# One load for the first K, beta and masks, V's scaling behind the first solve, later loads chained by copies, and another clock model in a self-ordered linear-attention and MoE kernel

## The chip, the cores and the metric

The kernel runs on one core of one Trainium2 chip. TensorE (PE) does the matmuls and loads their weights (PEld), VectorE (DVE, V in the code), ScalarE (ACT, A) and GpSimd (POOL, G) do the rest, and SyncE (SP) issues the DMAs. The metric is device time in microseconds, the median of several runs. The profile is of one further execution.

## The reference

Two parts follow each other: a delta-rule linear attention over 4 batches, 8 heads, 768 tokens and head size 48, and a gated feed-forward layer on its result.

```python
k_n = k / (norm(k) + 1e-6)
state = zeros(B, H, 48, 48)
for t in range(768):
    y[t] = q[t] @ state                      # read before the update
    v_old = state.T @ k_n[t]
    state += beta[t] * outer(k_n[t], v[t] - v_old)
x = y.transpose(0, 2, 1, 3).reshape(3072, 384)
out = ((x @ w_a) * (x @ w_b)) @ w_out        # 384 -> 1536 -> 384
```

## The kernel before

**Attention.** The 768 tokens are cut into 24 chunks (c) of 32, and four chunks make a group (g = 0 to 5). All 32 heads of a chunk are worked on together: 128 partitions hold four blocks of 32 tokens, and eight column blocks hold the rest. For each group there are three generators. `prep(g)` loads K (tile `knb`), the transposed keys and queries (`rawb`, from `in_kqt`) and V (`vnb`) of two pairs of chunks, squares K for its norms, forms `dc` (beta over the norm), multiplies keys with keys and queries for each chunk (the Gram matmuls `bank<-rawb`), writes the scaled Gram blocks into `gnat` (tile `b4`, shown as `b`) and the masked key-query products into `at`; then it sums squares of V and of the keys and queries for a power-of-two scale (`sc`, with one matmul against `ones`), and multiplies V by the norms (`vnb<-vnb,nm`). `solve(g)` transposes the Gram blocks and eliminates on VectorE, step by step (`tmp<-b,b`, then `b<-b,tmp`), transposes the result (`b`, `xn`), and in groups 0 and 1 completes it on TensorE (`bank<-b,tt`, `bank<-b,mk`, `wr`, `bank<-wr,xn`) into `tt`. `steps(g)` goes through the chunks: state times keys and queries (`bank<-sh,rawb`), `f` = V minus that, `u` from `tt` and `f`, the state update `S_ps<-u,knb`, and the outputs `bank<-u,at`, which become `y`, are transposed (`yt`) and split into two half-precision parts (`xb`).

**MoE.** `weights(i)` loads one of 12 blocks of the layer's weights (`in_w`, 1.15 MB) into `late` or a part of `wh` that is free, unpacks it on VectorE (one TENSOR_SCALAR and two SCALAR_TENSOR_TENSOR of 128x1152), forms a power-of-two scale (`sw`, with ScalarE's square and one matmul against `ones`), and writes high and low halves; for blocks 0 to 3 the low halves come from TensorE (`zi`, `neg`, `negr`). `moe(s, fcs)` then does a MoE unit for a pair of chunks s and a block fc: 18 matmuls `bank<-xb,wh`, ScalarE's copy `a`, the product `g`, its two halves `ghl`, and six matmuls `bank<-wo,ghl`. There are 12 pairs and 12 blocks, so 144 units.

**Order.** No instruction is issued while this code runs. Each call is recorded as an `Op` by a `Plan` (hence one line, 481, for nearly all rows of the profile), and `Plan.pack` then lists the operations: an engine takes the ready operation of highest priority, with priorities from six passes forwards and backwards. The planner's rules matter here: `price` gives durations, `fetch` models TensorE's instruction fetch in blocks of 256, a window of 3,413 ns models its clock (`warm`, `use`), and before 60 us gaps on TensorE are filled with idle matmuls on `ones` (line 472): small ones of 128x32 and large ones of 128x256, which the trace shows as two passes each. `plan.behind` puts an operation behind named others in the plan alone. Engines are in-order, so what stands ahead in an engine's list is waited for.

**Loads.** `EARLY` and `NEXT` give the first loads. In `NEXT`, a GpSimd copy of one element from an earlier load's target into the next one's makes the second DMA wait for the first one's landing. In groups 2 to 5 the loads of a group were only ordered in the plan.

Of the kernel before, what the change touches and what calls it, by code (L numbers as in the profile page):

```python
# [42 lines left out]

EARLY = [(0, "k"), (2, "k"), (0, "r"), (0, "b")]
NEXT = [(2, "r", 0, "k"), (0, "v", 0, "r"), (2, "v", 2, "r"), (0, "w", 2, "r"), (1, "w", 0, "v"), (2, "w", 2, "v"), (4, "k", 0, "w"), (4, "r", 1, "w"), (4, "v", 2, "w")]
QUEUE = [(0, [0, 1, 2, 3, 4, 5]), (1, [0, 1, 2, 3, 4, 5]), (0, [6, 7, 8]), (1, [6, 7, 8]), (0, [9, 10, 11]), (1, [9, 10, 11])]
# [14 lines left out]
class Plan:  # L61
# [131 lines left out]
    def add(self, eng, fn, name, args, kw):  # L193
# [73 lines left out]
    def pack(self, pri, back=False):  # L267
# [17 lines left out]
        while len(done) < n:  # L285
# [59 lines left out]
            if e == "PE" and not back:  # L345

                if kept:
                    f, end = max(free[e], self.SINCE), min(t - self.SHY, slow.get(i, t))
                    room = end - f
                    fill[i], best_ = [0, 0], None  # L350
                    for lot in range(int(room / self.IDLE[0]) + 1 if room > 3000.0 else 1):
                        p_, c_, f_, m = pos, come, f, 0
# [7 lines left out]
                    while True:  # L360
                        k = 0 if fill[i][0] + 1 <= n_small else 1
                        while until <= f:
                            warm = use > 0.43 * self.WINDOW if warm else use > 0.75 * self.WINDOW
                            use, until = 0.0, until + self.WINDOW
                        took = self.IDLE[k] * (1 if warm or not k else 2)
                        slip, past, then = self.fetch(f, 2 + 2 * k, took, pos, come, dma)
                        if slip > 1.0 or f + took > end:
                            break
                        use, f, pos, come = use + took, f + took, past, then
                        fill[i][k] += 1  # L370
                _, pos, come = self.fetch(t, o.words, o.dur if warm else o.cold, pos, come, dma)
                while until <= t:
                    warm = use > 0.43 * self.WINDOW if warm else use > 0.75 * self.WINDOW
                    use, until = 0.0, until + self.WINDOW
                took = o.dur if warm else o.cold
                full = took * o.use / o.dur
                part = min(1.0, (until - t) / took)
                use += full * part
                if part < 1.0:
                    warm = use > 0.43 * self.WINDOW if warm else use > 0.75 * self.WINDOW  # L380
                    use, until = full * (1 - part), until + self.WINDOW
# [28 lines left out]
    BEGIN, IDLE, SINCE, UNTIL = 63, (50.0, 440.0), 1200.0, 60e3  # L410
    SHY, AIM = 400.0, 56

    def fetch(self, t, n, took, pos, come, dma):
        slip, come = 0.0, come[:]
# [69 lines left out]
@with_exitstack  # L484
def tile_kernel(ctx, tc, kqt, kn, vn, beta, w, masks, out):
    nc = tc.nc
# [51 lines left out]
    rawb = one("rawb", [P, 6, 1024])  # L538
    knb = one("knb", [P, 6, 384])
    vnb = one("vnb", [P, 6, 384])  # L540
# [26 lines left out]

    mk = one("mk", [P, 32 + P + 2])
    parity = mk[:, 32 + P :]
    bt = one("bt", [P, NG * 32])  # L570
    amask = mk[:, 0:32]
# [108 lines left out]
    def target(c, what):  # L680
        t = {"b": lambda: bt, "w": lambda: slots[c].bitcast(F32), "k": lambda: knp(c)[:, 0], "v": lambda: vnp(c)[:, 0], "r": lambda: rawp(c)[:, 0]}
        return t[what]()[0:1, 0:1]

    def load(c, what):
# [3 lines left out]
        if what == "w":  # L688
            SP.dma_start(slots[c].rearrange("p (n d) -> p n d", n=4), w[c].bitcast(I32)[:, :, 0 : WB // 4])
        elif what == "b":  # L690
            SP.dma_start(bt, beta)
            SP.dma_start(mk, masks)
        elif what == "k":
            SP.dma_start(knp(c).rearrange("p c d -> p (c d)"), kn[c // 2])
        elif what == "v":
            SP.dma_start(vnp(c).rearrange("p c d -> p (c d)"), vn[c // 2])
        else:
            SP.dma_start(rawp(c).rearrange("p c (h d) -> p (c h) d", h=2), kqt[c // 2][:, :, 0:512])

    def prep(g):  # L700
        chs = GROUPS[g]
        ss = sst
        if g > 1:
            last = []
            for c in chs[2], chs[0]:
                for what in "krv":
                    plan.behind = set(last)
                    load(c, what)
                    last = [len(plan.ops) - 1]
        for c in chs[::2]:  # L710
# [22 lines left out]
        for ci, c in enumerate(chs):  # L733
# [21 lines left out]
            ats[c] = atr()  # L755
            V.tensor_mul(ats[c], ga[:, :, 32:64], amask.unsqueeze(1).broadcast_to([P, 8, 32]))
            yield
        sc = scr()
        V.memset(sc[:, 0:4], 0.0)
# [13 lines left out]
        if g:  # L773
            V.tensor_add(sc[:, 2:3], sc[:, 2:3], vsum[-1])
        V.tensor_add(sc[:, 2:3], sc[:, 2:3], sc[:, 3:4])
        V.tensor_add(sc[:, 0:1], sc[:, 0:1], sc[:, 1:2])
        vsum.append(sc[:, 2:3])
# [12 lines left out]
        for ci, c in enumerate(chs):  # L790
            facs[c] = fac
            (V if g < 2 else G).tensor_mul(
                vnc(c).rearrange("p (q e) -> p q e", e=D),
# [5 lines left out]
    def solve(g):  # L799
# [5 lines left out]
        V.transpose(dtt, dcs[g])  # L805
        X = b4().rearrange("p (a b) -> p a b", b=32)
        (G if g else V).memset(X, 0.0)
        V.tensor_copy(X.rearrange("p t s -> p (t s)")[:, 0 : 33 * 31 + 1 : 33], dtt)
# [306 lines left out]
def _layout(inputs):  # L1115
# [25 lines left out]
    for j in range(3):  # L1141
# [12 lines left out]
    wide = np.zeros((NFC, P, 4, 288 + 8), w.dtype)  # L1154
    wide[..., 0:288] = w.reshape(NFC, P, 4, 288)
    return {
        "kqt": pieces,
        "kn": f(natl(k)),
        "vn": f(natl(v)),
        "beta": f(bp.reshape(P, NG * 32)),  # L1160
        "w": wide.view(np.int64),
        "masks": masks,
    }
# [17 lines left out]
```

## Time and profile before

| what | value |
|---|---|
| median of 3 runs | 656.05 us (653.93 to 656.95) |
| profiled execution, its own time | 659.53 us |
| its span, first to last instruction | 657.5 us |
| mean granted TensorE clock | 0.984 |
| PE busy | 626.8 us (95%) |
| VectorE busy | 406.5 us (62%) |
| idle matmuls on `ones` | 165 records, 22.1 us |

The page shows busy time by engine, then 40 slices of 16.4 us each with busy tenths, granted clock (PEclk, 9 is 90% or more) and DMA. "Idle before, releaser" is the time an engine waited ahead of a row and what ended it; "issue" means nothing that the profile shows. A matmul of 32-bit floats counts as two matmuls and two weight loads.

### The profile page before, as it was taken

To read this page: it belongs to the slowest core of one execution; us is meant where nothing else is said; L and a number is where in the kernel's file an instruction comes from. 1 tells how busy PE (TensorE), PEld (TensorE's weight loads), DVE (VectorE), ACT (ScalarE), POOL (GpSimd) and SP (SyncE) were. 2 spreads that over 40 slices of the span, in tenths; PEclk is the share of its full clock that TensorE was granted. 3 is DMA by queue.
4 is the path that set the end of the run, shared out by engine and by line. 5 is a ranking of instruction groups with operands and counts; after the bars stand their busy time and mean duration, and the time that the engine had idled before them with its cause. 6 is when DMAs were issued, how large, how long until landed. Compare 5 with 4: busy or idle time off the path is not lost.

```text
span 657.5 us, 26749 instructions
## 1 busy us (share of the span) xinstructions
PE 626.8 (95%) x12297; PEld 534.1 (81%) x12297; DVE 406.5 (62%) x1059; ACT 271.7 (41%) x599; POOL 21.4 (3%) x34
## 2 busy tenths in 40 slices
PE   6899989999899999979999999999999989999997
PEld 5766778788788888868888788888888877888886
DVE  5888898876468974337974348954449844332222
ACT  3257854354374443314543326453322253332322
POOL 0000000000021100000200001100000000000000
PEclk9879999999899999979999999999999999999999
DMA  7848042024143000033000051000000000000000
GB/s 249 315 147 329 6 140 81 3 77 167 62 162 115 1 25 4 13 129 114 1 25 4 4 202 50 1 26 3 4 3 25 1 27 4 2 25 1 25 1 25
DMA packets 19985, 42.78 MB, mean 65 GB/s; under 512 B 1185, under 2 KB 4513, under 8 KB 19873
## 3 DMA queue, kind: packets, MB, share of 16 engines
q1 hardware_dynamic: 19872, 41.08, 17.7%
q8 instruction: 96, 1.57, 1.0%
q14 instruction: 17, 0.13, 0.1%
HBM read 36.36 MB, written 4.72 MB: 62 GB/s over the span
## 4 chain that ended last, share of the span: by engine, by line
PE 76%; DVE 15%; ACT 4%; issue 3%; DMA 2%; SPq 0%; POOL 0%; ACTq 0%; DVEq 0%
PE bank L481 70%; DVE b L481 5%; DVE tmp L481 3%; PE S_ps L481 3%; PE bank L472 2%; DVE ghl L481 2%; DVE g L481 1%; ACT tt L481 1%; DMA rawb<-in_kqt 1%; ACT ghl L481 1%; ACT sqf L481 1%; DMA vnb<-in_vn 1%; DVE f L481 0%; DVE late L481 0%; ACT a L481 0%
## 5 line engine op out<-in xcount | busy, mean ns | idle before, releaser
L481 PEld LDWEIGHTS <-wh 128*128 128x128 f16 x2592 | 242.8, 99 | 54.4 <-issue 24.3
L481 PE MATMUL bank<-xb,wh 128*128 128x256 f16 x2160 | 262.0, 275 | 4.8 <-issue 3.5
L481 PE MATMUL bank<-wo,ghl 128*128 128x384 f32 x864 | 191.5, 355 | 1.0 <-issue 1.0
L481 PEld LDWEIGHTS bank<-wo,ghl 128*128 128x128 f32 x864 | 145.1, 191 | 5.1 <-issue 1.2
L481 ACT COPY a<-bank 128x256 f32<-128x256 f32 x144 | 53.6, 372 | 202.0 <-PE bank L481 201.5
L481 DVE TENSOR_TENSOR g<-bank,a 128x256 f32<-128x256 f32 x144 | 60.6, 421 | 121.4 <-ACT a L481 120.5
L481 ACT CAST ghl<-g 128x256 fp32r<-128x256 f32 x144 | 58.1, 404 | 76.3 <-DVE g L481 75.8
L481 DVE TENSOR_TENSOR ghl<-g,ghl 128x256 fp32r<-128x256 f32 x144 | 62.5, 434 | 37.7 <-ACT ghl L481 35.3
L481 DVE TENSOR_TENSOR b<-b,tmp 128x31 f32<-128x31 f32 (+20 forms) x154 | 51.9, 337 | 3.1
L481 PE MATMUL bank<-late,wh 128*128 128x256 f16 x432 | 53.1, 273 | 0.1
L481 DVE TENSOR_TENSOR tmp<-b,b 128x31 f32<-128x31 f32 (+20 forms) x154 | 50.9, 331 | 2.9
L481 DVE SCALAR_TENSOR_TENSOR y<-bank,sc,y 128x384 f32<-128x384 f32 x23 | 14.2, 617 | 42.4 <-ACT y L481 40.9
L481 PE MATMUL bank<-rawb 48*32 48x64 f32 x1280 | 25.2, 236 | 9.0 <-DMA rawb<-in_kqt 4.9
L481 PEld LDWEIGHTS bank<-rawb 48*32 48x32 f32 x1280 | 22.1, 119 | 13.5 <-issue 5.8
L481 ACT COPY sh<-S_ps 112x768 f32<-112x768 f32 x23 | 18.4, 798 | 22.8 <-PE S_ps L481 22.6
L481 PEld LDWEIGHTS bank<-sh,rawb 48*64 48x64 f32 x1216 | 19.7, 134 | 6.2 <-issue 3.8
L481 PE MATMUL bank<-sh,rawb 48*64 48x48 f32 x1216 | 22.3, 220 | 1.6 <-issue 1.6
L481 PE MATMUL bank<-u,at 32*32 32x48 f32 x1536 | 21.8, 203 | 1.6 <-issue 1.6
L472 PE MATMUL bank<-ones 128*32 128x32 bf16 (+1 forms) x165 | 22.1, 292 | 1.1 <-DVE ones L481 1.1
L481 PEld LDWEIGHTS bank<-f,tt 32*32 32x32 f32 x1472 | 17.4, 105 | 6.8 <-issue 2.7
L481 PEld LDWEIGHTS bank<-u,at 32*32 32x32 f32 x1536 | 18.3, 105 | 4.8 <-issue 4.0
L481 PEld LDWEIGHTS S_ps<-u,knb 32*48 32x48 f32 x1216 | 16.2, 123 | 7.3 <-issue 4.2
(118 smaller groups left out, 538.3 us busy)
## 6 DMA issues: line engine op xcount, KB each, us to landing
late<-in_w SPq DMA_DIRECT2D x10, 1152.0 KB, 7.6
rawb<-in_kqt SPq DMA_DIRECT2D x10, 1024.0 KB, 7.9
out<-late SPq DMA_DIRECT2D x24, 192.0 KB, 1.9
knb<-in_kn SPq DMA_DIRECT2D x10, 384.0 KB, 6.5
vnb<-in_vn SPq DMA_DIRECT2D x10, 384.0 KB, 6.1
wh<-in_w SPq DMA_DIRECT2D x2, 1152.0 KB, 10.1
late<-in_kqt SPq DMA_DIRECT2D x2, 1024.0 KB, 6.2
late<-in_kn SPq DMA_DIRECT2D x2, 384.0 KB, 3.1
```

Source lines behind the costliest of these rows:

```text
L472: self.nc.tensor.matmul(self.pool[-1][0 : 32 + 96 * k, 0 : 32 + 224 * k], one, one.unsqueeze(1).broadcast_to([P, 1 + k, 32 + 96 * k])[:, 0 ...
L481: fn(*(self.place(a, lease) for a in args), **{k: self.place(a, lease) for k, a in kw.items()})
```

## The change

It has five parts. K of chunks 0 and 1, beta and the masks come in one load of 1,122 floats a partition into one tile `kb`, which also holds the later K; the second key-query load is gated by the second K instead of the first. In group 0 `prep` is split: the masked product `at` of chunk 3, the norm's sums, `sc` and V's scaling are put behind the first solve's last transpose, by generators and `plan.behind`. In groups 2 to 5 each load is chained to the one before it by a GpSimd copy, and the key-query loads are cut into halves (`r0`, `r1`). The planner's clock model counts use by the part of the array that a matmul fills, with thresholds `KEEP` and `GAIN` and other idle rules (`SHY`, `HEAT`). `fetch` no longer judges a block that it has only just added.

```diff
-EARLY = [(0, "k"), (2, "k"), (0, "r"), (0, "b")]
-NEXT = [(2, "r", 0, "k"), (0, "v", 0, "r"), ...
+EARLY = [(0, "k"), (2, "k"), (0, "r")]
+NEXT = [(2, "r", 2, "k"), (0, "v", 0, "r"), ...
...
-                op.use += dur
+                n = 1
+                for d in outs[0].shape[1:]:
+                    n *= d
+                k, m, f = ins[0].shape[0] / 128, ins[0].shape[-1] / 128, ins[0].dtype == F32
+                op.use += (1 + 3 * f) * n / 2.4 * m * (k + 1) / 2 + 5 * f
...
-                    for lot in range(int(room / self.IDLE[0]) + 1 if room > 3000.0 else 1):
+                    for lot in range(max(1, int((room - 4000.0) / self.IDLE[0]))):
...
-                            warm = use > 0.43 * self.WINDOW if warm else use > 0.75 * self.WINDOW
+                            warm = use > (self.KEEP if warm else self.GAIN) * self.WINDOW
...
-    SHY, AIM = 400.0, 56
+    SHY, KEEP, GAIN, HEAT = 1500.0, 0.41, 0.42, (3.0, 430.0)
...
-            slip = max(slip, come[b] - at)
+            if b < known:
+                slip = max(slip, come[b] - at)
...
-        elif what == "b":
-            SP.dma_start(bt, beta)
-            SP.dma_start(mk, masks)
+        elif what == "k" and c == 0:
+            SP.dma_start(kb[:, 0 : begin.shape[1]], begin)
...
-                for what in "krv":
-                    plan.behind = set(last)
-                    load(c, what)
-                    last = [len(plan.ops) - 1]
+                for part in "k", "r0", "r1", "v":
+                    if (c, part[0]) in loaded and part != "r1":
+                        continue
+                    if last:
+                        G.tensor_copy(target(c, part), target(*last))
+                    load(c, part)
+                    last = c, part
...
+        if g == 0:
+            yield
+            plan.lease.update(rest[1])
+            plan.behind = set(ready)
+            rest[0]()
...
+            plan.behind = set() if g else set(ready)
             (V if g < 2 else G).tensor_mul(
...
+        if g == 0:
+            ready[:] = [len(plan.ops) - 1]
+            yield
...
+    for _ in range(6):
+        next(pr[0])
+    for _ in range(4):
+        next(sv[0])
     run_all(pr[0])
     next(ws[0])
-    for _ in range(3):
-        next(sv[0])
```

TensorE, from the last of the 97 small idle matmuls up to the first solve's result (`b_3_71`), before: 

```order
L472 MATMUL bank_66<-ones 128x256
L481 MATMUL bank_61<-rawb 32x64 x32
L481 MATMUL bank_62<-rawb 32x64 x32
L481 MATMUL bank_63<-rawb 32x64 x32
L481 MATMUL bank_64<-rawb 32x64 x32
L472 MATMUL bank_66<-ones 128x256 x6
L481 MATMUL bank_65<-sc_129,ones 128x1 x2
L472 MATMUL bank_66<-ones 128x256 x21
L481 MATMUL bank_61<-b_3_71,tt_85 32x16 x32
```

The same place after, from TensorE's first instruction:

```order
L477 MATMUL bank_66<-ones 128x256 x6
L486 MATMUL bank_61<-rawb 32x64 x32
L486 MATMUL bank_62<-rawb 32x64 x32
L486 MATMUL bank_63<-rawb 32x64 x32
L486 MATMUL bank_64<-rawb 32x64 x32
L477 MATMUL bank_66<-ones 128x256 x20
L486 MATMUL bank_65<-b_3_71,tt_85 32x16 x32
L486 MATMUL bank_61<-b_3_71,tt_86 32x16 x32
L486 MATMUL bank_62<-sc_127,ones 128x1 x2
```

The small idle matmuls are gone, six large ones stand ahead of the Gram blocks, and the norm's product (`sc`) has moved behind the first two blocks of the solve's result.

VectorE, from the Gram block of chunk 2 to the first elimination steps, before:

```order
L481 TENSOR_TENSOR b_0_68<-bank_62,dc_124 128x8x32
L481 TENSOR_TENSOR at_78<-bank_62,mk 128x256
L481 TENSOR_TENSOR vnb<-vnb,nm_126 128x384 x2
L481 TENSOR_TENSOR b_0_68<-bank_63,dc_124 128x8x32
L481 TENSOR_TENSOR at_79<-bank_63,mk 128x256
L481 TENSOR_TENSOR b_0_68<-bank_64,dc_124 128x8x32
L481 TENSOR_TENSOR at_80<-bank_64,mk 128x256
L481 TENSOR_TENSOR sc_129<-sc_129 128x1
L481 TENSOR_TENSOR vnb<-vnb,nm_126 128x384 x2
L481 STREAM_TRANSPOSE b_1_69<-b_0_68 128x1024
L481 TENSOR_TENSOR sc_129<-sc_129 128x1
L481 TENSOR_TENSOR tmp<-b_1_69,b_2_70 128x30
```

And after:

```order
L486 TENSOR_TENSOR b_0_68<-bank_62,dc_122 128x8x32
L486 TENSOR_TENSOR at_78<-bank_62,kb 128x256
L486 TENSOR_TENSOR b_0_68<-bank_63,dc_122 128x8x32
L486 TENSOR_TENSOR at_79<-bank_63,kb 128x256
L486 TENSOR_TENSOR b_0_68<-bank_64,dc_122 128x8x32
L486 STREAM_TRANSPOSE b_1_69<-b_0_68 128x1024
L486 TENSOR_TENSOR tmp<-b_1_69,b_2_70 128x30
```

Both pairs of V's scalings, chunk 3's `at` and the sums of `sc` have left this stretch; they follow the solve's transposes, ahead of the first weights (`wh<-late`).

SP, the loads of groups 2 and 3 behind the last weights (`late<-in_w`), before:

```order
L481 DMA late<-in_kn 128x768
L481 DMA late<-in_kqt 128x4x512
L481 DMA late<-in_vn 128x768
L481 DMA knb<-in_kn 128x768
L481 DMA rawb<-in_kqt 128x4x512
L481 DMA vnb<-in_vn 128x768
L481 DMA knb<-in_kn 128x768
```

And after, where each waits for a copy on POOL:

```order
L486 DMA late<-in_kn 128x768
L486 DMA late<-in_kqt 128x2x512 x2
L486 DMA kb<-in_kn 128x768
L486 DMA late<-in_vn 128x768
L486 DMA rawb<-in_kqt 128x2x512
L486 DMA kb<-in_kn 128x768
L486 DMA rawb<-in_kqt 128x2x512 x2
```

The key-query loads have become halves, and the loads of group 3 (the first `kb<-in_kn`) now stand between those of group 2.

More of the change, by code (lines that the diff above doesn't have):

```diff
@@ L368, in pack @@
                             break
-                        use, f, pos, come = use + took, f + took, past, then
+                        use, f, pos, come = use + self.HEAT[k], f + took, past, then
                         fill[i][k] += 1
@@ L372, in pack @@
                 while until <= t:
-                    warm = use > 0.43 * self.WINDOW if warm else use > 0.75 * self.WINDOW
+                    warm = use > (self.KEEP if warm else self.GAIN) * self.WINDOW
                     use, until = 0.0, until + self.WINDOW
                 took = o.dur if warm else o.cold
-                full = took * o.use / o.dur
+                full = o.use
                 part = min(1.0, (until - t) / took)
@@ L379, in pack @@
                 if part < 1.0:
-                    warm = use > 0.43 * self.WINDOW if warm else use > 0.75 * self.WINDOW
+                    warm = use > (self.KEEP if warm else self.GAIN) * self.WINDOW
                     use, until = full * (1 - part), until + self.WINDOW
@@ L410 @@
     BEGIN, IDLE, SINCE, UNTIL = 63, (50.0, 440.0), 1200.0, 60e3
-    SHY, AIM = 400.0, 56
+    SHY, KEEP, GAIN, HEAT = 1500.0, 0.41, 0.42, (3.0, 430.0)
     def fetch(self, t, n, took, pos, come, dma):
-        slip, come = 0.0, come[:]
+        slip, come, known = 0.0, come[:], len(come)
         for b in range(-(-pos // 256), -(-(pos + n) // 256)):
             at = t + took * (b * 256 - pos) / n
-            slip = max(slip, come[b] - at)
+            if b < known:
+                slip = max(slip, come[b] - at)
             if b + 1 == len(come):
@@ L484, in tile_kernel @@
 @with_exitstack
-def tile_kernel(ctx, tc, kqt, kn, vn, beta, w, masks, out):
+def tile_kernel(ctx, tc, kqt, kn, vn, begin, w, out):
     nc = tc.nc
@@ L538, in tile_kernel @@
     rawb = one("rawb", [P, 6, 1024])
-    knb = one("knb", [P, 6, 384])
+    kb = one("kb", [P, NG * 32 + 32 + P + 2 + 6 * 384])
+    bt = kb[:, 0 : NG * 32]
+    mk = kb[:, NG * 32 : NG * 32 + 32 + P + 2]
+    knb = kb[:, NG * 32 + 32 + P + 2 :].rearrange("p (c d) -> p c d", d=384)
     vnb = one("vnb", [P, 6, 384])
@@ L566, in vnc @@
         return vnp(c // 2 * 2)[:, c % 2]
-    mk = one("mk", [P, 32 + P + 2])
     parity = mk[:, 32 + P :]
-    bt = one("bt", [P, NG * 32])
     amask = mk[:, 0:32]
@@ L680, in target @@
     def target(c, what):
-        t = {"b": lambda: bt, "w": lambda: slots[c].bitcast(F32), "k": lambda: knp(c)[:, 0], "v": lambda: vnp(c)[:, 0], "r": lambda: rawp(c)[:, 0]}
+        t = {"w": lambda: slots[c].bitcast(F32), "k": lambda: knp(c)[:, 0], "v": lambda: vnp(c)[:, 0], "r": lambda: rawp(c)[:, 0], "r0": lambda: rawp(c)[:, 0], "r1": lambda: rawp(c)[:, 1]}
         return t[what]()[0:1, 0:1]
@@ L696, in load @@
             SP.dma_start(vnp(c).rearrange("p c d -> p (c d)"), vn[c // 2])
-        else:
-            SP.dma_start(rawp(c).rearrange("p c (h d) -> p (c h) d", h=2), kqt[c // 2][:, :, 0:512])
+        elif what == "r":
+            SP.dma_start(rawp(c).rearrange("p c (h d) -> p (c h) d", h=2), kqt[c // 2][:, :, 0:512])
+        else:
+            i = int(what[1])
+            loaded.add((c, "r"))
+            SP.dma_start(rawp(c)[:, i].rearrange("p (h d) -> p h d", h=2), kqt[c // 2][:, 2 * i : 2 * i + 2, 0:512])
     def prep(g):
@@ L755, in prep @@
             ats[c] = atr()
-            V.tensor_mul(ats[c], ga[:, :, 32:64], amask.unsqueeze(1).broadcast_to([P, 8, 32]))
-            yield
+            if c == 3:
+                rest = partial(V.tensor_mul, ats[c], ga[:, :, 32:64], amask.unsqueeze(1).broadcast_to([P, 8, 32]))
+                rest = rest, {t.tensor.name: plan.lease[t.tensor.name] for t in [ga]}
+            else:
+                V.tensor_mul(ats[c], ga[:, :, 32:64], amask.unsqueeze(1).broadcast_to([P, 8, 32]))
+            yield
+        if g == 0:
[3 more added lines that the diff above has]
+            rest[0]()
         sc = scr()
@@ L774, in prep @@
             V.tensor_add(sc[:, 2:3], sc[:, 2:3], vsum[-1])
+        plan.behind = set() if g else set(ready)
         V.tensor_add(sc[:, 2:3], sc[:, 2:3], sc[:, 3:4])
+        plan.behind = set() if g else set(ready)
         V.tensor_add(sc[:, 0:1], sc[:, 0:1], sc[:, 1:2])
@@ L791, in prep @@
             facs[c] = fac
+            plan.behind = set() if g else set(ready)
             (V if g < 2 else G).tensor_mul(
@@ L806, in solve @@
         X = b4().rearrange("p (a b) -> p a b", b=32)
+        plan.behind = set(ready if g else ())
         (G if g else V).memset(X, 0.0)
@@ L1155, in _layout @@
     wide[..., 0:288] = w.reshape(NFC, P, 4, 288)
+    nat = f(natl(k))
     return {
         "kqt": pieces,
-        "kn": f(natl(k)),
+        "kn": nat,
         "vn": f(natl(v)),
-        "beta": f(bp.reshape(P, NG * 32)),
+        "first": f(np.concatenate([bp.reshape(P, NG * 32), masks, nat[0]], axis=1)),
         "w": wide.view(np.int64),
-        "masks": masks,
     }
```

2 lines of the change are left out of this document (1 added, 1 removed).

## The prediction

> **What bounds the kernel now.** First the page: how long, which engine, at what clock.
>
> ```profile
> span 657.5 us, 26749 instructions
> PE 626.8 (95%) x12297; PEld 534.1 (81%) x12297; DVE 406.5 (62%) x1059; ACT 271.7 (41%) x599; POOL 21.4 (3%) x34
> PEclk9879999999899999979999999999999999999999
> q8 instruction: 96, 1.57, 1.0%
> ```
>
> TensorE is the bound over the whole span. The change can therefore gain only where TensorE idles, repeats idle work, or runs at a lower clock: 30.7 us of idle, and the slices with digits 7 and 8. The last row counts 96 fetches of 16 KB for PE's 24,594 instructions, 256 to each. Next the stages of the beginning (PE, PEld, DVE, ACT, POOL busy, then granted clock, DMA share, GB/s):
>
> ```profile
> 0.00:9.80 9.80, 3.92 (x99) 3.17 (x99) 3.95 (x9) 3.40 (x5) 0.38 (x5) 1.00 0.81 267
> ...
> 33.30:65.00 31.70, 29.48 (x831) 20.26 (x831) 27.00 (x52) 20.58 (x43) 1.04 (x1) 0.89 0.68 245
> ```
>
> VectorE is busy 27.0 of 31.7 us before the first MoE product at 65 us: there it is the bound beside TensorE, with 4.7 us of idle. The chain of waits says what sets 33.3 us, where TensorE starts on the first solve's result:
>
> ```profile
> 21.91 0.60 PE bank L481 x4
> 22.51 10.86 PE bank L472 x42
> 33.37 2.90 PE bank L481 x172
> ```
>
> The norm's product (21.91) and 42 idle passes behind it on the in-order TensorE stand ahead of 33.37. VectorE's order in the same stretch:
>
> ```profile
> 17.71 0.58 DVE L481 TENSOR_TENSOR b<-bank,dc 128x256 f32<-128x256 f32 x1
> 19.31 1.03 DVE L481 TENSOR_TENSOR vnb<-vnb,nm 128x384 f32<-128x384 f32 x2
> 20.26 1.24 DVE L481 STREAM_TRANSPOSE b<-b 128x1024 f32<-128x1024 f32 x1
> 21.77 0.18 DVE L481 TENSOR_TENSOR tmp<-b,b 128x30 f32<-128x30 f32 x1
> 30.61 1.25 DVE L481 STREAM_TRANSPOSE b<-b 128x1024 f32<-128x1024 f32 x1
> 31.78 1.03 DVE L481 STREAM_TRANSPOSE xn<-b 128x512 f32<-128x512 f32 x1
> 32.73 2.22 DVE L481 TENSOR_SCALAR wh<-late 128x1152 int32<-128x1152 int32 x2
> 42.42 0.16 DVE L481 TENSOR_SCALAR sw<-bank 128x1 int32<-128x1 int32 x1 [1.74 <-PE bank L481]
> ```
>
> V's scaling (vnb) stands between the last Gram block (17.71) and its transpose. Behind the start, the waits of TensorE with "issue" as releaser are 12.9 us, and two are long, each with a slow clock behind it:
>
> ```profile
> PE bank L481 <- issue: 12.9, 10, 3.3
> 173.28 1.79 PE L481 MATMUL bank<-xb,wh 128*128 128x256 f16 x8 [1.83 <-issue]
> 173.30:176.70 3.40, 3.40 (x14) 2.78 (x14) 1.13 (x3) 1.19 (x3) 0.00 (x0) 0.52 0.02 5
> 280.00:285.00 5.00, 3.93 (x134) 3.23 (x132) 2.68 (x6) 1.19 (x3) 0.00 (x0) 1.00 0.95 333
> 287.26 0.43 PE L481 MATMUL bank<-rawb 48*32 48x64 f32 x6 [3.33 <-issue]
> 287.30:292.90 5.60, 5.60 (x29) 4.39 (x29) 1.26 (x3) 0.67 (x2) 0.00 (x0) 0.50 0.02 7
> 346.80:375.40 28.60, 27.76 (x942) 22.91 (x940) 12.90 (x27) 10.27 (x22) 0.00 (x0) 1.00 0.02 4
> ```
>
> The gap of 3.33 us follows 5 us in which the DMA engines are 95% busy; I read it as an instruction fetch behind those loads. The last row is a dense stretch of small matmuls: 942 in 28.6 us, 33 a microsecond or some 3.9 us for 256 instructions, at an idle DMA. I take that as the pace that fetches allow.
>
> **The change, part by part.**
>
> *First load with beta and masks.* It puts 177 KB ahead of the first key-query load and takes two issues from SP. At 267 GB/s that is 0.66 us later at most, and nothing at least, since those bytes were moved in the same stretch behind it. I take 0.4. The second key-query load starts after K of chunks 2 and 3 has landed, yet it stood behind the first one anyway: between 0 and the 1.5 us that 384 KB take at 267 GB/s, taken as 0, for the stage's row shows the DMA engines 81% busy.
>
> *Fillers.* 97 small and one large before the attention's first matmuls become six large, and 27 behind them become 20. The small ones used up instructions, so that the next fetch started early. Without them the second boundary falls into the fourth Gram block: -0.4 to +0.7 us at its end (17.0), taken as 0. Rows for the cold and the warm rate:
>
> ```profile
> 9.84 7.19 PE L481 MATMUL bank<-rawb 48*32 48x64 f32 x256 [4.87 <-DMA rawb<-in_kqt]
> 88.41 1.10 PE L481 MATMUL bank<-rawb 48*32 48x64 f32 x64
> 287.62 4.02 PE L481 MATMUL bank<-xb,wh 128*128 128x256 f16 x18
> 75.96 2.14 PE L481 MATMUL bank<-xb,wh 128*128 128x256 f16 x18
> ```
>
> The first blocks take 28 ns a matmul against 17 later, so TensorE is cold up to 17 us. The six large ones, 12 passes at twice the 0.26 us of a warm one (10.86 / 42), end near 7 us, and 3 us of idle follow before 9.84, so I expect the first blocks cold again. The Trainium skill's page "TensorE: Matmul & The Clock Gate" (section "What's actually happening") says that half clock is the default and a busy window of about 3.4 us releases it; the half-clock rows above agree (3.4 and 5.6 us). By it the six fillers would warm the array and one idle window would lose it again, which is the same sum.
>
> *V's scaling behind the solve.* Last Gram block at 17.2 to 17.8, transpose to 19.1, first elimination step at 19.1 for 21.77: 2.7 us earlier. The elimination itself keeps its 8.84 us (30.61 - 21.77) less some 0.2 for the norm's steps that leave it. Its first transpose ends at 29.0 for 31.86. On TensorE 40 passes stand between 17.0 and there: at 0.26 us (10.86 / 42) 10.4 us, to 27.4; with two cold windows, up to 30.9. So TensorE starts on the result between 29.2 and 30.9 for 33.30, taken 29.5.
>
> *What is late next: VectorE.* At the solve's end it now has one mask product (under the 0.58 of the Gram product), four scalings (2 x 1.03) and the norm's chain of ten short steps (0.16 each, as at 42.42), which used to hide inside the solve. The solve's two transposes end at 30.0, so weights begin at 33.1 (if the short steps fit between the scalings) to 34.4, for 32.73. Taken: 1.0 later. Its idle up to 65 us is 4.7; the 1.74 at 42.42 goes at least, since three weights are now unpacked before the first norm is waited for; taken 3.2. The sixth weight's unpacking is done at 65.3 before; after it is 65.3 + 1.0 + 1.0 (one more pair of f) - 3.2 = 64.1; with ScalarE's square and the norm (1.3) the first MoE product stands at 65.4. That is as late as before, but the order puts more of the attention ahead of it:
>
> ```profile
> 64.99 0.27 PE L481 MATMUL bank<-xb,wh 128*128 128x256 f16 x1
> 70.97 0.74 PE L481 MATMUL bank<-b,tt 32*32 32x16 f32 x64
> 72.64 1.03 PE L481 MATMUL bank<-b,mk 128*128 128x256 f32 x2
> 74.58 0.88 PE L481 MATMUL bank<-f,tt 32*32 32x48 f32 x64
> 75.28 0.74 PE L481 MATMUL bank<-wr,xn 32*16 32x16 f32 x64
> 83.27 1.15 PE L481 MATMUL bank<-sh,rawb 48*64 48x48 f32 x64
> ```
>
> One each of b,tt, b,mk, f,tt and sh and two of wr, less the pipelining at their ends, but with a zi product and small ones: 0.74 + 1.03 + 0.88 + 1.15 + 1.48 = 5.3, taken 5.4 us, done early. Gain 65.0 + 5.4 - 65.4 = 5.0; with the other ends of both VectorE terms 2.7 to 7.1. The fetch pace bounds it: about 1,150 matmuls stand between the solve's result and the first MoE product, 1,150 / 33 = 35 us after 29.5, or 64.5, hence at most 5.9. Less the 0.4 of the first load: **head -4.6 us** (-2 to -6).
>
> *Loads chained by copies.* From group 2 on each load waits for the one before it, key-query loads in halves: 28 more copies on POOL (3% busy) and six more issues on SP. A link is one landing, a copy and an issue:
>
> ```profile
> late<-in_kn SPq DMA_DIRECT2D x2, 384.0 KB, 3.1
> rawb<-in_kqt SPq DMA_DIRECT2D x10, 1024.0 KB, 7.9
> ```
>
> ```profile
> 21.83 0.17 POOL L481 COPY knb<-late 1x1 f32<-1x1 f32 x1 [4.30 <-DMA late<-in_w]
> 22.03 0.33 SPq L481 DMA_DIRECT2D knb<-in_kn  x1
> ```
>
> ```profile
> 639.57 2.14 PE L481 MATMUL bank<-xb,wh 128*128 128x256 f16 x18
> ...
> 642.61 2.14 PE L481 MATMUL bank<-xb,wh 128*128 128x256 f16 x18
> ```
>
> 3.6 us at an idle DMA; 8.4 if each took what full key-query loads take among others. In group 2 V of pair 10 stands on SP behind K of chunk 14, which waits for chunk 7's state product; three links later the first Gram block needs its half, 10.8 us, and the order has six MoE units (642.61 - 639.57 = 3.04 us each), a sh and a u block (2 us) ahead of it, 20.2 us in all: hidden. The stretch at 280 us then has gaps between transfers, and the 3.33 us with its half clock (5.6 x 0.5 = 2.8) should mostly go: -5. The gap at 173 us (1.83 + 3.4 x 0.48 = 3.5 in all) had no load beside it and may stay or move; the new order has as many dense stretches and may form another: +1.5. **Middle -3.5 us** (-9.6 if all goes, +2 if more gaps form).
>
> *Clock model.* It only moves rows; what it moves is counted above.
>
> Sum: -8.1 us on the profiled execution, 657.5 to 649.4. Its own time is 659.5 and lies 3.5 above the median of the runs, 656.05; on the median's scale 656.05 - 8.05 = **648.0 us**.
>
> **The rivals.** *Loads were not the cause.* The gaps come from dense matmuls and re-form elsewhere: only the head remains, 651.5. For it speaks the gap at 173 us beside an idle DMA; against it the 95%. The Trainium skill's page "Runtime: NRT & Kernel Launch" (section "Instruction fetch mechanics") calls crossing a 16 KiB boundary "mostly hidden", so that spacing loads would bring nothing; the 12.9 us of issue gaps disagree.
>
> *All of it.* Both gaps and all of VectorE's idle go: -6 and -7, 643.
>
> *A wash.* Norm and scaling delay the weights by 1.7, VectorE's idle stays, and the links take 8.4 us, so that the group's first block waits 5 us (3 x 8.4 - 20.2) and the clock drops (2.8): -2 + 7.8 - 5, 656.9.
>
> *Slower: a cold array.* After 30 us no filler is left, while before three stretches of them stood there. Some 26.5 us of matmuls lie between 29.5 and 65.4; at the cold rate, 1.63 (28 / 17) to 1.88 (4.02 / 2.14) times, they take 43 to 50 us, so the first MoE product comes 7 to 14 us later: up to 662. It decides above 1.78 times, a mean clock below 0.56 from 30 to 65 us. Against it: 0.89 before, with few fillers.
>
> **How the numbers follow.** About 0.5% is what runs of this kernel tell from no change: 652.8 to 659.3. Forecast 0.46 (645 to 651); loads not the cause 0.22 (650.5 to 653.5, a third of it above 652.8); all of it 0.10; a wash 0.12; cold 0.10. Faster 0.46 + 0.15 + 0.10 = 0.71; same 0.07 + 0.11 = 0.18; slower 0.11. From 642 to 656 leaves out most of the last case, half of the wash's upper side and little below: under 2 in 10.
>
> **What would show it.** Right: first elimination step near 19, TensorE on the solve's result near 29.5, weights near 33.7, no gap over 2 us behind a load, PEclk without a 7 at 280 us. Wrong: a first MoE product after 68, half clock between 30 and 65, new gaps with issue as releaser that sum to over 12 us, or a Gram block of group 2 waiting for its load.

## The result, and the profile after

The changed kernel is slower: 659.29 us median of 13 runs (657.73 to 662.6) against 653.12 us of 13 runs of the kernel before (650.49 to 656.95), a ratio of 1.0088 with a 95% interval of 1.0064 to 1.0112. The forecast was 648.0. The profiled execution took 659.57 us.

The page of the changed kernel:

```profile
span 657.8 us, 26608 instructions
...
PE 627.5 (95%) x12184; PEld 533.6 (81%) x12184; DVE 405.0 (62%) x1059; ACT 271.5 (41%) x599; POOL 26.0 (4%) x62
...
PEclk8858999979999999999999999999999999999999
```

TensorE is as busy as in the profile of before (626.8 us), though 113 records are gone. The 7 at 280 us has gone too, and a 5 and a 7 stand in the third and ninth slice. The granted clock there, by windows (columns as in the prediction):

```profile
30.87:54.76 23.89, 21.16 (x654) 16.03 (x640) 17.76 (x46) 11.87 (x24) 0.95 (x1) 0.50 0.52 180
129.85:140.09 10.24, 9.23 (x155) 7.05 (x156) 3.83 (x13) 3.23 (x5) 0.00 (x0) 0.50 0.30 112
```

Half clock for 23.9 us in one piece behind the first solve, and again for 10.2 us in group 1. VectorE in the head:

```profile
18.62 0.60 DVE L486 TENSOR_TENSOR b<-bank,dc 128x256 f32<-128x256 f32 x1 [3.19 <-ACT tt L486]
...
20.54 0.19 DVE L486 TENSOR_TENSOR tmp<-b,b 128x30 f32<-128x30 f32 x1
...
35.33 1.43 DVE L486 TENSOR_SCALAR wh<-late 128x1152 int32<-128x1152 int32 x2
```

The elimination starts at 20.54 (21.77 before), not at 19.1: VectorE waits 3.19 us for ScalarE, whose copy of the fourth Gram block (`tt`) stands behind squares in ScalarE's order. The weights begin at 35.33 (32.73 before). TensorE's rows with a wait of 1 us or more ahead, from the solve's result up to 160 us, and the first MoE product:

```profile
30.59 1.75 PE L486 MATMUL bank<-b,tt 32*32 32x16 f32 x128 [3.48 <-DVE b L486]
...
39.01 0.78 PE L486 MATMUL bank<-vnb,tt 32*32 32x48 f32 x27 [1.66 <-issue]
...
66.18 0.34 PE L486 MATMUL bank<-wh,neg 128*128 128x384 f16 x1 [2.26 <-issue]
...
75.79 2.13 PE L486 MATMUL bank<-xb,wh 128*128 128x256 f16 x18
...
100.69 0.26 PE L486 MATMUL bank<-sh,rawb 48*64 48x48 f32 x2 [1.04 <-issue]
120.22 0.24 PE L486 MATMUL bank<-b,tt 32*32 32x16 f32 x3 [1.21 <-issue]
132.44 1.03 PE L486 MATMUL bank<-f,tt 32*32 32x48 f32 x41 [1.01 <-issue]
154.17 0.71 PE L486 MATMUL bank<-xb,wh 128*128 128x256 f16 x5 [1.75 <-issue]
```

The row at 75.79 is the first MoE product (64.99 before); it has no wait ahead. From 30.59 to there stand 1,148 matmuls, the 1,150 of the prediction, but they take 45.2 us where it had 35. Between the gaps from 66.18 on, the windows count these matmuls:

```profile
66.18:100.68 34.50, 32.32 (x1020) 25.79 (x1021) 29.57 (x75) 26.63 (x57) 0.00 (x0) 1.00 0.11 37
100.69:120.21 19.52, 18.31 (x255) 15.91 (x255) 17.55 (x60) 6.33 (x15) 0.00 (x0) 1.00 0.19 62
120.22:132.43 12.21, 10.71 (x256) 7.60 (x256) 8.29 (x15) 4.36 (x11) 0.00 (x0) 0.89 0.52 187
132.44:154.16 21.72, 19.98 (x512) 16.53 (x512) 14.48 (x32) 10.30 (x22) 0.00 (x0) 0.82 0.19 63
```

With a weight load for each matmul that is 2,040, 510, 512 and 1,024 instructions, or 8, 2, 2 and 4 times 256 but for a few missing records. So the gaps stand whole blocks of 256 instructions apart, the size of a fetch. The profile doesn't show what TensorE waits for there; that it is the fetch is read from this spacing. In what follows a boundary is a place where such a block ends. All such waits of TensorE sum to 13.1 us (12.9 before), of which 7.2 are the five rows from 39.01 to 132.44; the first and the last of these lie in the two half-clock windows.

### The profile page after: what moved, and what is told of

The parts are those of the page before. It is cut to its first block, busy times and chain, and to the rows that moved or that the text cites. A ratio compares the mean times of both kernels' runs of the same rounds, so it can differ in the third digit from the quotient of the medians.

```text
span 657.8 us, 26608 instructions
## 1 busy us (share of the span) xinstructions
PE 627.5 (95%) x12184; PEld 533.6 (81%) x12184; DVE 405.0 (62%) x1059; ACT 271.5 (41%) x599; POOL 26.0 (4%) x62
## 4 chain that ended last, share of the span: by engine, by line
PE 67%; DVE 14%; ACT 5%; issue 3%; DMA 0%; POOL 0%; ACTq 0%
PE bank L486 64%; DVE b L486 4%; DVE tmp L486 3%; PE S_ps L486 3%; DVE ghl L486 2%; DVE g L486 2%; ACT tt L486 1%; ACT ghl L486 1%; ACT sqf L486 1%; ACT a L486 1%; DVE late L486 0%; DMA vnb<-in_vn 0%; DVE wh L486 0%; ACT u L486 0%; DVE s L486 0%
## 5 line engine op out<-in xcount | busy, mean ns | idle before, releaser
L486 DVE TENSOR_TENSOR tmp<-b,b 128x31 f32<-128x31 f32 (+20 forms) x154 | 52.5, 341 | 2.8
L486 PEld LDWEIGHTS bank<-rawb 48*32 48x32 f32 x1280 | 20.7, 113 | 9.1 <-issue 4.9
L486 PEld LDWEIGHTS bank<-f,tt 32*32 32x32 f32 x1472 | 18.1, 107 | 10.2 <-issue 4.4
L486 PE MATMUL bank<-f,tt 32*32 32x48 f32 x1472 | 21.6, 206 | 3.4 <-ACT tt L486 1.3
L486 ACT COPY sh<-S_ps 112x768 f32<-112x768 f32 x23 | 18.4, 799 | 14.2 <-PE S_ps L486 14.1
L486 ACT COPY u<-bank 128x384 f32<-128x384 f32 x24 | 11.4, 475 | 25.7 <-PE bank L486 25.6
```

What stands on the lines that cost most here:

```text
L486: fn(*(self.place(a, lease) for a in args), **{k: self.place(a, lease) for k, a in kw.items()})
```

## The experiments

Ratios are to runs of the kernel before that shared the chip, with 95% intervals. "Small" and "large" are the idle matmuls on `ones`.

| run | small/large ahead of Gram, behind it | ratio |
|---|---|---|
| changed kernel | 0/6, 0/20 | 1.0088 (1.0064 to 1.0112) |
| e2 | 0/6, 0/28 | 1.0092 (1.0058 to 1.0126) |
| e3 old clock model | 97/2, 0/28 | 0.9978 (0.9950 to 1.0007) |
| e4 unchained | 0/6, 0/20 | 1.0094 (1.0059 to 1.0129) |
| e5 order of e3 | 0/6, 0/20 | 1.0028 (1.0001 to 1.0055) |
| e6 | 97/1, 0/28 | 0.9899 (0.9864 to 0.9933) |
| e7 V's scaling in place | 0/6, 0/13 | 0.9973 (0.9949 to 0.9997) |
| e8 first load and chain | 97/2, 0/24 | 0.9896 (0.9853 to 0.9938) |
| e9 | 0/6, 32/20 | 1.0132 (1.0081 to 1.0183) |
| e10 | 0/6, 64/20 | 0.9987 (0.9950 to 1.0025) |
| e11 | 0/6, 103/20 | 0.9899 (0.9865 to 0.9932) |
| e12 | 97/1, 41/20 | 1.0103 (1.0052 to 1.0154) |
| e13 e11 without links | 0/6, 103/20 | 0.9895 (0.9871 to 0.9919) |
| e14 e11, scaling back | 0/6, 103/20 | 0.9966 (0.9946 to 0.9986) |
| e15 before, 32 more | 129/1, 0/27 | 1.0068 (1.0039 to 1.0097) |
| e16 before, 64 more | 161/1, 0/27 | 1.0051 (1.0021 to 1.0082) |
| e17 e11, copy first | 0/6, 123/10 | 0.9869 (0.9831 to 0.9907) |

**e1: the kernel before again**, unchanged.

> The kernel before, unchanged, profiled a second time. Theory A (the 3.33 us stall at 284 us and its half clock belong to that one profiled execution, not to most runs): no gap over 2 us between 270 and 300 us, no granted half clock there, and a span of about 651 us, 6 us under the 657.5 first profiled. Rival B (the stall is in most runs): a gap of about 3 us at the same matmul again, and a span near 657.

One run, 652.56 us, span 650.5. Theory A's span came, but not its reason. TensorE near 280 us in this execution:

```profile
283.45 0.31 PE L481 MATMUL bank<-rawb 48*32 48x64 f32 x6 [3.89 <-issue]
```

The stall stands in both profiles of the kernel before; what the first had more was elsewhere (its gap of 1.83 us at 173 us, 1.19 here, with the slow clock behind it, and a first MoE product at 64.99 where this one has it at 62.46).

**e2: eight more large idle matmuls** in the wait for the solve.

```diff
+    warmed = False
...
+                if self.ops[i].eng == "PE" and self.ops[i].stream == "solve0" and not self.warmed:
+                    self.warmed = True
+                    self.fill[i][1] += 8
```

> The changed kernel with every instruction in its place, and 8 more large idle matmuls on TensorE (28 instead of 20) behind the first Gram matmuls, in the 3.48 us in which TensorE waits for the first solve's result. Theory A (the cold array costs the head 3 to 4 us): the half clock from 30.9 to 54.8 us goes or shrinks to one or two windows, the first MoE product comes 3 to 4 us earlier, and the time falls from 1.009 to about 1.003 of the kernel before. Rival B (VectorE's later start sets the head, and the slow clock only fills TensorE's waiting time): the half clock goes, but the first MoE product moves by less than 1.5 us and the ratio stays at 1.007 to 1.010. Rival C (sparse small matmuls can't hold the clock whatever comes before them): half clock returns by 40 us and the ratio stays.

1.0092: no gain. The slow clock came back at 40 us, rival C:

```profile
40.00:57.00 17.00, 14.69 (x380) 10.56 (x383) 11.32 (x29) 10.68 (x20) 0.00 (x0) 0.50 0.82 296
```

The eight also add 32 instructions, so this run moves the boundaries too and is no clean test of the clock.

**e3: the old clock model; e4: unchained loads.** e3 takes back the rules of `use`, `KEEP`, `GAIN`, `HEAT`, `SHY` and `fetch`; e4 takes back the loop over `"k", "r0", "r1", "v"` (both as in the front diff, reversed).

> The changed kernel with the clock model, filler rules and fetch rule of the kernel before: first load, V's scaling and chained loads stay, the small idle matmuls come back. Theory A (the clock model's rules, by taking the idle matmuls away between 27 and 55 us and by putting dense attention earlier, are the loss): ratio 0.990 to 1.000, no half clock over 7 us between 30 and 60 us. Rival B (V's scaling behind the solve is the loss, by delaying the weights 2.6 us): ratio 1.006 or more.

> The changed kernel with the loads of groups 2 to 5 ordered in the plan only, as before, and no copies on GpSimd; TensorE's order is the same up to the end of group 1's attention. Theory A (most runs have no stall behind the loads, so chaining gains nothing): ratio 1.006 to 1.012 of the kernel before, as with the chain. Rival B (chaining removes 3 to 6 us of stalls): ratio 1.014 or more, with gaps over 2 us behind loads from group 2 on. Rival C (chaining costs time): ratio 1.004 or less.

e3 gave 0.9978, theory A: with the old rules the loss is gone. e4 gave 1.0094, theory A: without the chain nothing is measurably worse. Its trace does have a gap of 1.72 us at 300 us, where the changed kernel has none.

**e5 and e6: order against idle matmuls.** The new rules change two things, the order of real work and the idle matmuls. Both kernels set the idle matmuls by hand, with the rest of each order as it was:

```diff
         self.bind, self.fill = best[4]
+        lots = [i for i in best[3] if ops[i].eng == "PE"]
+        gram = [i for i in lots if ops[i].stream == "prep0"][:4]
+        self.fill = {lots[0]: [0, 6], lots[lots.index(gram[3]) + 1]: [0, 20]}      # e5, on e3
+        self.fill = {lots[0]: [97, 1], lots[lots.index(gram[3]) + 1]: [0, 28]}     # e6, on the changed kernel
```

> The order of all real work as the old clock model gives it (the kernel of the run before with 0.998), but with the idle matmuls of the changed kernel: 6 large ones ahead of the first Gram block and 20 behind the fourth, none of the 97 small ones. Theory A (the order that the new clock model gives is the loss): 0.995 to 1.001 of the kernel before. Theory B (the idle matmuls are the loss, by the cold array behind them and by the 98 fewer matmuls that move every instruction fetch): 1.005 to 1.010, with 20 us or more of half clock in one stretch between 30 and 55 us.

> The mirror of it: the changed kernel's order of real work, with 97 small and one large idle matmul ahead of the first Gram block and 28 behind the fourth. Theory A (order): 1.006 to 1.012, and the half clock between 30 and 55 us and at 130 to 140 us stays. Theory B (idle matmuls): 0.995 to 1.001, and both go.

Theory B on the changed kernel's order, and beyond its range: 1.0088 became 0.9899 (647.92 us median) with no real instruction moved. Theory B's other sign came only in part: the granted clock is still 0.50 from 128 to 134 us. On the old order e5 lies between its two theories; against e3 the exchange costs 0.5%, with intervals that just meet. TensorE's waits in e6:

```profile
PE bank L489 <- issue: 3.7, 5, 1.4
```

13.1 us of gaps have become 3.7.

**e7 and e8: parts of the change in other company.** e7 takes back V's scaling (the generators' `yield`s and `plan.behind`), e8 that and the clock model.

> The changed kernel with V's scaling, the norm and the last masked product back ahead of the first solve; first load, chain and new clock model stay. Theory A (the clock model is the loss whatever stands in the head): 1.004 to 1.010. Theory B (moving V's scaling makes the loss together with the new model, by the wait of 3.5 us for the solve with no idle matmul left in it): 0.995 to 1.001, with no half-clock stretch over 10 us before 65 us.

> Only the first load with beta and masks and the chained loads, with V's scaling in its old place and the old clock model. Theory A (the chain removes the gap of 3.3 to 3.9 us at 280 us, which both profiles of the kernel before show, and nothing else moves): 0.990 to 0.995, with no gap over 2 us and no half clock between 270 and 300 us. Theory B (the gap comes back elsewhere): 0.997 to 1.003.

0.9973 and 0.9896. Both order all work anew, so they price no part: by now it was clear that the boundaries move with any edit. They show that the new model isn't bound to lose (e7, although its clock is 0.50 from 33.6 to 46 us, against theory B's sign), and that first load and chain stand in a kernel with 1% gained (e8, whose gap at 280 us is gone).

**e9 to e12: the boundaries alone.** The idle matmuls are, besides work, 2 instructions (small) or 4 (large). e9, e10 and e11 put 32, 64 and 103 small ones ahead of the 20 large ones behind the fourth Gram block, which moves each later boundary by 64, 128 or 206 instructions. e12 has the small ones ahead of the Gram blocks as e6 has, and enough behind to move boundaries by 256, that is not at all.

```diff
+        self.fill = {lots[0]: [0, 6], lots[lots.index(gram[3]) + 1]: [N, 20]}      # N = 32, 64, 103
+        self.fill = {lots[0]: [97, 1], lots[lots.index(gram[3]) + 1]: [41, 20]}    # e12
```

> The changed kernel, every instruction kept, with 32 small idle matmuls (some 36 ns each, 1.2 us in all) ahead of the 20 large ones behind the fourth Gram block, where TensorE idles 3.48 us anyway. They add 64 instructions, so that every later boundary of 256 falls 64 instructions earlier in the real work. Theory P (what the 98 idle matmuls were worth is the place of the boundaries): the time changes by more than 2 us although nothing else does; the issue gaps (13.1 us in the changed kernel) change with it. Theory W (it is the small ones' work ahead of the first Gram block, or the warmth): 1.006 to 1.012 as before.

> The same with 64 small ones, 128 instructions, half a block. Theory P: another time again, with other issue gaps; the time follows the sum of the issue gaps (3.7 us at 0.990, 13.1 at 1.009). Theory W: 1.006 to 1.012.

> The same with 103 small ones, 206 instructions: behind the solve every boundary falls where it fell in the run with 0.990, yet ahead of the first Gram block there are only the 6 large ones. Theory P: 0.988 to 0.994, issue gaps under 6 us. Theory W: 1.006 or more.

> The changed kernel with 97 small and one large idle matmul ahead of the first Gram block and 41 small and 20 large behind the fourth: 256 instructions more than the changed kernel, so that each boundary behind the solve falls where it falls in the changed kernel, one block on. Theory P: 1.005 to 1.012, with issue gaps over 10 us at the same matmuls as in the changed kernel. Theory W (the small ones ahead are what helps): 0.988 to 0.994.

Theory P: 1.0132, 0.9987, 0.9899, 1.0103. e9 alone would not show it, for its interval overlaps the changed kernel's; e10 and e11 lie clear of the changed kernel, and e12 is back at it. The waits of TensorE (us in total, times, longest) in e9, then e10, then e11 (the second row is its idle matmuls' own wait), then e12:

```profile
PE bank L489 <- issue: 14.7, 13, 3.5
```

```profile
PE bank L489 <- issue: 6.3, 5, 2.7
```

```profile
PE bank L489 <- issue: 4.6, 4, 2.1
PE bank L480 <- issue: 2.9, 1, 2.9
```

```profile
PE bank L489 <- issue: 14.1, 13, 2.4
```

Within this order the ratio rises with the sum, though not in proportion (3.7 us in e6, 4.6, 6.3, 13.1, 14.1, 14.7). And e12, with 256 instructions more, has its gaps ahead of the very matmuls at which the changed kernel has them, down to the counts of the rows:

```profile
40.24 0.78 PE L489 MATMUL bank<-vnb,tt 32*32 32x48 f32 x27 [1.18 <-issue]
66.66 0.34 PE L489 MATMUL bank<-wh,neg 128*128 128x384 f16 x1 [2.35 <-issue]
102.13 0.26 PE L489 MATMUL bank<-sh,rawb 48*64 48x48 f32 x2 [0.86 <-issue]
122.23 0.29 PE L489 MATMUL bank<-b,tt 32*32 32x16 f32 x3 [1.76 <-issue]
135.26 1.03 PE L489 MATMUL bank<-f,tt 32*32 32x48 f32 x41 [1.15 <-issue]
156.75 0.71 PE L489 MATMUL bank<-xb,wh 128*128 128x256 f16 x5 [1.67 <-issue]
```

A rival is the array's warmth when the solve's result arrives. The idle matmuls of e11 run right up to it; those of e9, e12 and e10 end 4.4 to 5.5 us ahead, in this order:

```profile
30.64 1.96 PE L489 MATMUL bank<-b,tt 32*32 32x16 f32 x128 [5.51 <-DVE b L489]
```

```profile
32.15 1.91 PE L489 MATMUL bank<-b,tt 32*32 32x16 f32 x128 [4.68 <-DVE b L489]
```

```profile
32.06 1.61 PE L489 MATMUL bank<-b,tt 32*32 32x16 f32 x128 [4.44 <-DVE b L489]
```

Warmth alone doesn't fit: e10 idles longer there than the changed kernel (3.48 us) and is 1% faster, and e6 idles 2.80 us and equals e11. Nor is the head where most of the time goes. In e11 the first MoE product, with as many matmuls ahead of it (1,149), comes only 1.9 us before the changed kernel's 75.79, of 11.1 us by which the spans differ (657.8 less 646.7):

```profile
73.92 2.13 PE L489 MATMUL bank<-xb,wh 128*128 128x256 f16 x18
```

So, with the order of the real work held, the time is shown to hang on where the boundaries fall in it. From e11 to the changed kernel it is 1.9% or 12 us (1.0088 less 0.9899, of 654). The sums of the gaps differ by 8.5 us (13.1 less 4.6). By the pages, 7.6 of the 11.1 us are idle time of TensorE (30.3 less 22.7) and 3.5 are busy time (627.5 less 624.0), although e11 has 103 matmuls more:

```profile
PE 624.0 (96%) x12287; PEld 533.1 (82%) x12287; DVE 404.7 (63%) x1059; ACT 271.3 (42%) x599; POOL 26.4 (4%) x62
```

The busy part I put down to the slow clock, which no run separates from the gaps: from 30 to 65 us the granted clock puts these kernels in the same order (0.60 in e9, 0.66 in the changed kernel and e12, 0.71 in e10, 0.76 in e11, 0.80 in e6).

**e13: the chain with boundaries held.** The copies that chain the loads are dropped when e11 is issued; SP's and all other orders stay.

```diff
+                if self.ops[i].tag == "link":
+                    continue
...
+                        plan.ops[-1].tag = "link"
```

> The run with 103 small idle matmuls (0.990), every instruction of TensorE, VectorE, ScalarE and SyncE kept in its place; only the copies on GpSimd that chain the loads of groups 2 to 5 are left out, so that loads start as soon as their target is free. Theory L (loads in a crowd delay the instruction fetch): 0.995 to 1.000, with an issue gap over 2 us or a half-clock window between 225 and 320 us. Theory N (the chain itself does nothing, the order in which it was planned did): 0.988 to 0.993.

0.9895 against e11's 0.9899: the copies do nothing measurable. One gap near 280 us has come back, at a third of its size in the kernel before:

```profile
288.69 0.80 PE L491 MATMUL bank<-sh,rawb 48*64 48x48 f32 x40 [1.26 <-issue]
```

**e14: V's scaling with boundaries held.** On e11, seven operations go back ahead of the solve's transpose on VectorE, eight short ones into the elimination, and the norm's product on TensorE behind six of the 20 large ones.

```diff
+        late = [i for i in todo[cut:] if ops[i].stream == "prep0"]
...
+        early = [i for i in late if i not in steps]
+        todo = [i for i in todo if i not in late]
+        cut = todo.index(head[3])
+        todo[cut:cut] = early
+        for n, i in enumerate(steps):
+            todo.insert(todo.index(head[6 + 3 * n]) + 1, i)
```

> The run with 103 small idle matmuls (0.990), with the last masked product, the norm's sums and V's scaling moved back on VectorE ahead of the first solve, the norm's chain spread through the elimination, and the norm's product on TensorE behind 6 of the 20 large idle matmuls; all other orders are kept, and TensorE's boundaries behind the solve fall where they fell. The forecast's step (moving the scaling is worth 4.2 us): 0.996 or more. Rival (VectorE does the same work before the weights either way, and the solve's result comes 3 us later while the weights begin earlier): 0.988 to 0.992, weights begin within 1 us of the run with 103.

0.9966, 0.67% or 4.4 us above e11, with an uncertainty of some 2.5 us from the two intervals. VectorE in e11, then in e14:

```profile
21.32 0.19 DVE L489 TENSOR_TENSOR tmp<-b,b 128x30 f32<-128x30 f32 x1
...
35.76 1.43 DVE L489 TENSOR_SCALAR wh<-late 128x1152 int32<-128x1152 int32 x2
```

```profile
23.08 0.19 DVE L503 TENSOR_TENSOR tmp<-b,b 128x30 f32<-128x30 f32 x1
...
25.50 0.16 DVE L503 TENSOR_SCALAR sc<-bank 128x2 int32<-128x2 int32 x1 [1.74 <-PE bank L503]
...
35.61 2.23 DVE L503 TENSOR_SCALAR wh<-late 128x1152 int32<-128x1152 int32 x2
```

The weights begin at the same time, as the rival said, yet the time is longer, as the expectation's first case had it. TensorE's start on the solve's result tells why, first e11, then e14:

```profile
31.88 1.30 PE L489 MATMUL bank<-b,tt 32*32 32x16 f32 x128
```

```profile
34.82 1.90 PE L503 MATMUL bank<-b,tt 32*32 32x16 f32 x128 [3.20 <-DVE b L503]
...
48.85 0.41 PE L503 MATMUL S_ps<-u,kb 32*48 32x48 f32 x7 [2.97 <-issue]
```

2.9 us later, and a new gap of 2.97 us at a boundary behind it. The wait of 1.74 us for the norm's product belongs to my arrangement, so I put the part's worth between 2.7 (4.4 less 1.74) and 4.4 us, give or take the 2.5.

**e15 and e16: the kernel before, its boundaries moved.**

```diff
         self.bind, self.fill = best[4]
+        self.fill[[i for i in best[3] if ops[i].eng == "PE"][0]][0] += 32    # e16: 64
```

> The kernel before with 32 more small idle matmuls ahead of the first Gram block, where TensorE idles over 4 us: its boundaries fall 64 instructions earlier. If the kernel before hangs on its boundaries too: the time moves by more than 3 us, and the gap of 3.3 to 3.9 us at 280 us shrinks under 2 us or moves. If its gap is the loads' alone: 0.997 to 1.003 and the gap stays.

> The same with 64 more, half a block. If the kernel before hangs on its boundaries: another time again, by more than 3 us from the unshifted or the one with 32. If not: 0.997 to 1.003.

1.0068 and 1.0051: the kernel before stood at a better place than either. And loads beside it alone don't make its stall at 280 us: in e15 the boundary falls 32 matmuls earlier in the same Gram block, and the wait is a tenth of its size, although the loads run as before (DMA 88% busy). The longest gap of e15, 4.10 us, stands at 60.6 us.

```profile
293.40 0.76 PE L482 MATMUL bank<-rawb 48*32 48x64 f32 x38 [0.33 <-issue]
```

```profile
287.00:293.00 6.00, 5.59 (x157) 4.60 (x145) 3.45 (x7) 2.27 (x5) 0.00 (x0) 1.00 0.88 287
```

**e17: ScalarE's copy ahead of the squares**, on e11, with 20 idle matmuls more and 10 large ones fewer, the same count of instructions.

```diff
+        self.fill = {lots[0]: [0, 6], lots[lots.index(gram[3]) + 1]: [123, 10]}
...
+        todo.remove(copy)
+        todo.insert(todo.index(gram) + 1, copy)
```

> The run with 103 small idle matmuls (0.990), with ScalarE's copy of the fourth Gram block put ahead of two squares, so that VectorE doesn't wait 3.19 us for it, and with 123 small and 10 large idle matmuls instead of 103 and 20 behind the fourth Gram block: the same count of instructions, some 3 us shorter, so that TensorE is free when the solve ends. If the solve's start is on the path: first elimination step 2 to 2.5 us earlier, 0.985 to 0.988. If TensorE's clock or VectorE's later work takes it back: 0.989 to 0.993.

0.9869 (644.77 us median of 6), within the first expectation, though its interval overlaps that of e11. The elimination starts 2.9 us earlier than in e11:

```profile
16.52 0.60 DVE L494 TENSOR_TENSOR b<-bank,dc 128x256 f32<-128x256 f32 x1 [1.14 <-ACT tt L494]
...
18.44 0.19 DVE L494 TENSOR_TENSOR tmp<-b,b 128x30 f32<-128x30 f32 x1
```

By its median it is the fastest version here, 1.3% under the kernel before: the changed kernel with 123 small idle matmuls, 10 large ones fewer and one copy moved. The run doesn't part the copy's share from the idle matmuls'.

## Why the prediction was wrong

**The step that failed is "Fillers ... taken as 0".** I followed the removed instructions only to the second boundary, at the fourth Gram block, and priced that at -0.4 to +0.7 us, a range for which the prediction shows no row. There it was right: the changed kernel waits 0.28 us in that block. But their count moves every boundary of the next 600 us. The exchange of idle matmuls alone is worth 0.9899 against 1.0088, about 12 us, on a forecast of -8.1.

**The 648.0 was luck.** With the boundaries where the old idle matmuls put them, the same change gives 647.92 (e6) and 648.35 (e11). But the sum that gave 648.0 does not hold there either. Its head of -4.6 us rests on a first MoE product at 65.4; e6 has it at 72.87 and e11 at 73.92, since its 1,150 matmuls or so take 41.1 and 42.0 us there, not the 35 that the pace of 33 a microsecond gave. Its middle of -3.5 us had another cause (below). What e6 has less of than the kernel before is gaps: 3.7 us, against 12.9 and 12.5 in the two profiles of that kernel.

**Against the kernel before, the clock counts.** The gaps of the changed kernel sum to no more than those of the kernel before (13.1 against 12.9), and e16, with 10.3, is slower than the unshifted one; so across kernels of different order the sum tells little. TensorE's idle time is equal too, 30.3 us against 30.7 in e1. Its busy time differs, 627.5 against 619.8 us, with fewer idle matmuls in it and at a mean granted clock of 0.966 against 0.988. The line of e1:

```profile
PE 619.8 (95%) x12297; PEld 528.7 (81%) x12297; DVE 406.2 (62%) x1059; ACT 271.9 (42%) x599; POOL 21.4 (3%) x34
```

The new order runs on a slower clock in every placing of the boundaries (0.979 in e6, 0.973 in e11); with few gaps it gains all the same, with many it loses. How much each is worth no run shows.

**First load.** Expected 0.4 us late; the first Gram blocks start at 8.77 instead of 9.84. In the other kernels with the new load they start at 8.6 to 9.4 without small idle matmuls ahead and at 9.3 to 9.9 with them (9.80 in e6), so some of it may be the idle matmuls' doing. Their start was also quicker, 18 ns a matmul (0.93 / 52) where I had 28:

```profile
8.77 0.93 PE L486 MATMUL bank<-rawb 48*32 48x64 f32 x52 [2.23 <-DMA rawb<-in_kqt]
```

The granted clock was 1.00 there and 0.50 from 10.4 us on. (The prediction called the first blocks of the kernel before cold by their 28 ns; the clock in that profile reads 1.00 from 9.84 to 17.03.) The early start was not kept: the fourth block waited for ScalarE's order, a queue that the step had not followed.

**V's scaling behind the solve.** With boundaries held it gains, but less than forecast: 5.0 us (2.7 to 7.1) before the first load's 0.4 was taken off, 2.7 to 4.4 found, give or take 2.5. In the changed kernel only 1.2 of the 2.7 us at the elimination's start came, for the ScalarE copy; e17 has 3.3. The weights' delay was larger than I took (35.33 against 33.1 to 34.4).

**Loads chained by copies.** The stall at 280 us has gone, as forecast, but the reason given is at most part of it. I read a fetch delayed by loads that are 95% busy; in e15 a shift of the boundaries takes the stall away with the loads untouched. Dropping the copies brings back a gap that the chained twin lacks, 1.26 us (e13) and 1.72 us (e4), with no change in the ratio that can be told from noise. The Trainium skill's page "Runtime: NRT & Kernel Launch" (section "Instruction fetch mechanics") has the blocks of 256 instructions right by the counts above; its "mostly hidden" doesn't hold where small matmuls are dense, since here moving the crossings moves the time by 2.3% (0.9899 to 1.0132).

**The rivals.** "Loads were not the cause", by which gaps come from dense matmuls and re-form elsewhere, was nearest to what the gaps did; it had no price for more of them. "A cold array" had its signs: half clock from 30.87 us, and the first MoE product 10.4 us behind the forecast's 65.4. But the mean clock from 30 to 65 us was 0.66, above the 0.56 below which it was to decide. And e14 is hardly warmer in the head than the changed kernel, yet its time is 1.2% lower; first the changed kernel, then e14:

```profile
30.00:60.00 30.00, 26.36 (x802) 19.35 (x803) 22.59 (x52) 14.15 (x30) 0.95 (x1) 0.60 0.48 170
```

```profile
30.00:60.00 30.00, 21.51 (x668) 15.80 (x667) 20.05 (x48) 11.86 (x24) 1.47 (x1) 0.62 0.41 141
```

So the slow stretch in the head does not decide alone. Of the signs against me, "new gaps with issue as releaser that sum to over 12 us" came (13.1), but as written it could not tell a loss, since the kernel before already had 12.9. TensorE waits for a DMA only twice, 2.9 us in all, at the first blocks of group 0; no Gram block of group 2 does.

**The scale.** I put the profiled execution 3.5 us above a median of three runs; with 13 runs it is 6.4 us above (659.5 less 653.1), so the stated sum also began too high.

## What to carry to other kernels

Where TensorE runs thousands of short instructions, as here, count instructions and not only microseconds: an edit that adds or drops a few of them early moves every later boundary, and a comparison of two versions then measures the boundaries along with the edit. Hold the count modulo the block (here by idle matmuls in a wait that is there anyway) before pricing a part, and try a few shifts when the rest is settled. Where a stage is moved forward, follow each engine's queue to the last operand, ScalarE's copies among them.

## What the runs showed of the hardware

One kernel with 64, 128, 206 and 256 extra instructions early on gave 1.0132, 0.9987, 0.9899 and 1.0103, a spread of 2.3% with every real instruction in its place; the kernel before spans 0.7% over three places. And a busy TensorE was not granted the full clock: from 30.87 to 54.76 us of the changed kernel it was busy for 21.2 of 23.9 us with 654 mostly small matmuls, at 0.50 throughout; with 28 large idle matmuls ahead (e2) it was 0.50 again from 40 to 57 us.
